# Half-block weight loads behind each early pair, four-tick pairs, ungated loads for the third batch, and two queues for the last stores

## The chip, the cores and the metric

One Trainium2 chip, one of its cores. The metric is the device time of one execution in microseconds (us), as the median of several runs. One execution of the kernel before was also recorded by the hardware profiler; every duration in this document that is not a run's time comes from that record or from the record of an experiment.

The engines are named as the profile names them: PE (TensorE, matmuls), PEld (its weight loads), DVE (VectorE), ACT (ScalarE), POOL (GpSimd) and SP (SyncE, which here only issues transfers).

## The reference, cut to what matters

Two layers are fused. The first is attention over 8 batches with 8 heads, a sequence of 576 and a head width of 64. Heads 0 to 3 use a local mask, heads 4 to 7 a strided one:

```python
rel = pos[:, None] - pos[None, :]
mask_local = (rel >= 0) & (rel < 32)
mask_strided = (rel >= 0) & (pos[None, :] % 32 == pos[:, None] % 32)
attn = softmax(where(mask, q @ k.T / 8, -1e9)); x = attn @ v
```

The heads are laid side by side as x of 576 x 512. The second layer mixes along the sequence with a rank of 32, then along the channels:

```python
u = x + (x.T @ U @ V).T
out = u + relu(u @ w_ch1) @ w_ch2        # 512 -> 2048 -> 512
```

U, V, w_ch1 and w_ch2 arrive as float64 and are turned into float32 on the chip.

## The kernel before, in words

**The main stage.** The output rows are cut into nine pieces of 512: the first 512 rows of each of the eight batches, and a ninth piece made of the 64 last rows of all eight. For each piece the 2048 hidden channels are walked in 16 blocks of 128, so there are 144 steps. A step's first product (`gemm1`, L633) makes one 128 x 512 block of hidden values `ph` from 12 matmuls; ACT and DVE split its relu into a high part `gh` (L637) and a low part `gl` (L638); the second product (`gemm2`, L650) adds 12 matmuls to four accumulators `acc`. The loop runs `gemm1` of the next block before `gemm2` of the last, so each step is 24 matmuls. Work for the next batch is slipped in by `advance`, in half-steps called slots, 32 to a piece.

**The weights.** Block `fc` of both weight matrices is one load of 128 x 1024 float64 words (1 MB, `load_weights`, L155): columns 0 to 511 are what `gemm1` needs, columns 512 to 1023 what `gemm2` needs. `weights` (L171) converts it: `to_f32` scales the high words on ACT (L123) and puts the bits together on DVE (L125, L126, L128), into a buffer `cv`; then ACT writes the high part (L183) and DVE the low part (L184). The first five blocks (`N_FIRST`) are converted during the early attention, in two halves of one load. Each load of blocks 1 to 6 is held back by `load_behind` (L165): a one-word copy on POOL (L159) from a pair's probabilities into the load's buffer makes the load wait for that pair's exponential.

**The early attention.** Batches 0 and 1 (`NSP` is 2) are computed before the main stage by `first_attention` (L549) as eight pairs of heads (pairs 0 to 3 are batch 0, in the order 2, 3, 0, 1 of head pairs). A pair (`early_pair`, L215) loads `qk` and `v`, makes the scores on PE (L323, L329), subtracts the row maximum on DVE (L338, L339), takes the exponential on ACT (L343), transposes it on PE and copies it out on ACT (L350, L353, the tile `PT`), multiplies by v on PE (L363) and normalises on DVE (L372 to L379). For batch 0 it then runs `quarter` (L252): transposes of x, the rank-32 product and its split on PE, ACT and DVE, ending in `uh` and `ul` (L286, L287), the inputs of `gemm1`. The pairs are staggered by ticks, five to a pair of batch 0 and four to a pair of batch 1. All of it shares three banks of PSUM that are handed round. The four `quarter`s of batch 1 run inside the first steps of the main stage.

**The third batch and those after it.** For batches 2 to 7 the local heads run on PE inside the steps (`local_pairs`), and the strided heads on POOL and DVE (`strided_heads`, L404): 27 products on POOL (L422), each reduced on DVE (L424), a softmax, and 27 more products (L450) with their reductions (L452). `S0` names the slot in which a batch's strided heads begin. ACT then copies the result into place (L467, L471), after which SP loads the next batch's `st` into the same buffer (L408). Each instruction queue runs in order, so a `gl` that stands behind a reduction on DVE waits for that reduction's POOL product. For the third batch, `load_qk` and `load_v` hold the loads back by a one-word POOL copy (L201, L208).

**The end.** `finish` (L653) adds the accumulators to u on DVE (L656) and stores the result. For the ninth piece these are eight stores of 64 rows, all issued by SP.

The order on each engine is not written out by hand: a scheduler places the instructions as they are traced, `tc.issue_after` adds an order on one engine (the engine of the named instruction) and nothing between engines.

Of the kernel before, what the change touches and what calls it, by code (L numbers as in the profile page):

```python
# [22 lines left out]
CLA = 5  # L23
N_FIRST = 5
# [4 lines left out]
S0 = {2: 12, **{b: 32 * (b - 1) - 12 for b in range(3, 8)}}  # L29
# [6 lines left out]
def fused_kernel(ctx, tc, pairs, strided, U, V, w_in, masks, eye, out):  # L36
# [126 lines left out]
    gates = {}  # L163

    def load_behind(fc, word):  # L165

# [4 lines left out]
    def weights():  # L171
        for fc in range(NFC):
            load_ahead(fc + 1)
            cv = half_buffer(1024, "cv")
# [4 lines left out]
            fv = cv.rearrange("p (i x) -> p i x", i=2)
            yield  # L180
            parts = w_parts[fc] = const.tile([128, 2, 2, 512], F32R, name=f"w{fc}", tag=f"w{fc}")
            for x in range(2) if fc < N_FIRST else [slice(0, 2)]:
# [1 line left out]
                nc.vector.tensor_tensor(out=parts[:, x, 1], in0=fv[:, x], in1=parts[:, x, 0].bitcast(F32), op=ALU.subtract)  # L184
            yield
# [624 lines left out]
```

## Time and profile before

| What | Value |
|---|---|
| Median of 3 runs (lowest to highest) | 947.96 us (947.95 to 948.24) |
| The profiled execution's own time | 945.37 us |
| Its span, first to last instruction | 943.6 us |
| Mean granted TensorE clock | 0.992 |
| PE busy | 908.2 us, 96% of the span |
| PEld, DVE, ACT, POOL busy | 728.1, 562.0, 244.6, 325.2 us |
| Moved by transfers | 74.24 MB, 79 GB/s over the span |
| First-product matmuls L633 (1152 + 576), mean of one | 393 and 392 ns |
| Second-product matmuls L650 (1152 + 576), mean of one | 392 and 393 ns |

Matmuls overlap, so the mean of one is longer than the distance from one to the next. A row of the timeline gives a start, a duration, engine, line, operation and tiles, and in brackets the idle time before it with what ended it. The stretches view gives, for each window of time, the busy time of each engine, then the granted clock, the share of time that the 16 DMA engines were busy, and GB/s. A row of the chain of waits is a start, a duration and what the end of the program waited for at that moment.

### The profile page before, as it was taken

To read this page: it belongs to the slowest core of one execution; us is meant where nothing else is said; L and a number is where in the kernel's file an instruction comes from. 1 tells how busy PE (TensorE), PEld (TensorE's weight loads), DVE (VectorE), ACT (ScalarE), POOL (GpSimd) and SP (SyncE) were. 2 spreads that over 40 slices of the span, in tenths; PEclk is the share of its full clock that TensorE was granted. 3 is DMA by queue.
4 is the path that set the end of the run, shared out by engine and by line. 5 is a ranking of instruction groups with operands and counts; after the bars stand their busy time and mean duration, and the time that the engine had idled before them with its cause. 6 is when DMAs were issued, how large, how long until landed. Compare 5 with 4: busy or idle time off the path is not lost.

```text
span 943.6 us, 16802 instructions
## 1 busy us (share of the span) xinstructions
PE 908.2 (96%) x7032; PEld 728.1 (77%) x7032; DVE 562.0 (60%) x899; ACT 244.6 (26%) x481; POOL 325.2 (34%) x364
## 2 busy tenths in 40 slices
PE   5878999999989999999999999999999999999996
PEld 3656788777867778777887888778877888888885
DVE  4697997756786678666776677657764341122111
ACT  3454451214122412142114221421242121121110
POOL 0213307333853376346644565447440000000000
PEclk9998999999999999999999999999999999999998
DMA  9978001200240014101420142013300230001001
GB/s 349 382 248 325 1 26 62 96 1 8 74 164 24 12 59 161 49 1 58 139 71 1 51 156 72 1 51 106 112 2 1 56 114 22 0 1 46 1 1 45
DMA packets 35772, 74.24 MB, mean 79 GB/s; under 512 B 5840, under 2 KB 20560, under 8 KB 32880
## 3 DMA queue, kind: packets, MB, share of 16 engines
q1 hardware_dynamic: 25776, 67.13, 20.3%
q10 hardware_dynamic: 8960, 3.68, 1.6%
q0 software_dynamic: 960, 2.36, 0.8%
q8 instruction: 55, 0.90, 0.4%
q14 instruction: 21, 0.17, 0.1%
HBM read 54.14 MB, written 11.67 MB: 70 GB/s over the span
## 4 chain that ended last, share of the span: by engine, by line
PE 88%; DVE 5%; POOL 3%; DMA 1%; ACT 1%; issue 1%; SPq 0%; DVEq 0%; POOLq 0%; ACTq 0%
PE acc L650 40%; PE ph L633 39%; POOL tmp L422 3%; PE px L363 1%; PE px L329 1%; PE px L350 1%; DVE st L452 1%; DMA xg<-in_U_dram 1%; PE px L493 1%; DMA st<-in_strided_dram 1%; PE px L516 1%; PE acc L299 0%; PE px L299 0%; DVE late L339 0%; PE px L265 0%
## 5 line engine op out<-in xcount | busy, mean ns | idle before, releaser
L633 PE MATMUL ph<-uh,w 128*128 128x512 f32 x1152 | 383.3, 393 | 0.0
L650 PE MATMUL acc<-w,gh 128*128 128x512 f32 x1152 | 354.1, 392 | 0.0
L633 PEld LDWEIGHTS ph<-uh,w 128*128 128x128 f32 x1152 | 216.7, 188 | 47.2 <-issue 0.8
L650 PEld LDWEIGHTS acc<-w,gh 128*128 128x128 f32 x1152 | 215.5, 188 | 45.4
L638 DVE SCALAR_TENSOR_TENSOR gl<-ph,gh 128x512 fp32r<-128x512 f32 x144 | 98.7, 687 | 227.4 <-ACT gh L637 226.9
L633 PE MATMUL ph<-ul,w 128*128 128x512 f32 x576 | 225.9, 392 | 0.0
L650 PE MATMUL acc<-w,gl 128*128 128x512 f32 x576 | 219.9, 393 | 2.8 <-DVE gl L638 2.8
L637 ACT ACTIVATE gh<-ph 128x512 fp32r<-128x512 f32 x144 | 85.8, 597 | 469.7 <-PE ph L633 377.8
L450 POOL TENSOR_TENSOR tmp<-st,s_st 128x448 f32<-128x448 f32 (+7 forms) x162 | 136.5, 871 | 185.6 <-DVE st L452 98.6
L422 POOL TENSOR_TENSOR tmp<-st 128x576 f32<-128x576 f32 (+6 forms) x162 | 171.3, 1092 | 79.5 <-DMA st<-in_strided_dram 57.2
L452 DVE TENSOR_REDUCE st<-tmp 128x64 f32<-128x64 f32 (+8 forms) x162 | 137.4, 880 | 15.5 <-POOL tmp L450 14.3
L650 PEld LDWEIGHTS acc<-w,gl 128*128 128x128 f32 x576 | 108.1, 188 | 27.4 <-DVE gl L638 4.0
L633 PEld LDWEIGHTS ph<-ul,w 128*128 128x128 f32 x576 | 108.6, 189 | 22.8
L424 DVE TENSOR_REDUCE s_st<-tmp 128x9 f32<-128x576 f32 (+6 forms) x162 | 87.6, 563 | 24.5 <-POOL tmp L422 23.5
L467 ACT COPY xg<-st 32x256 f32<-32x256 f32 x96 | 38.8, 404 | 7.3 <-DVE st L452 5.8
L504 DVE TENSOR_TENSOR ta<-px,ta 32x256 f32<-32x256 f32 x36 | 15.1, 420 | 35.5 <-ACT ta L502 34.7
L656 DVE TENSOR_TENSOR xg<-acc,xg 128x512 f32<-128x512 f32 x36 | 22.9, 681 | 9.6 <-PE acc L650 9.6
L183 ACT CAST w<-cv 128x1024 fp32r<-128x1024 f32 (+1 forms) x21 | 17.3, 846 | 20.5 <-DVE cv L128 20.4
L625 DVE TENSOR_TENSOR ul<-raw,uh 128x512 fp32r<-128x512 f32 x32 | 20.8, 675 | 2.7 <-ACT uh L624 2.7
L518 DVE TENSOR_TENSOR xg<-px,xg 128x512 f32<-128x512 f32 x24 | 15.4, 685 | 11.6 <-PE px L516 11.6
L126 DVE SCALAR_TENSOR_TENSOR cv<-w,cv 128x1024 int32<-128x1024 int32 (+1 forms) x21 | 21.7, 1042 | 0.2
L184 DVE TENSOR_TENSOR w<-cv,w 128x1024 fp32r<-128x1024 f32 (+1 forms) x21 | 19.8, 962 | 2.6 <-ACT w L183 2.6
(152 smaller groups left out, 488.4 us busy)
## 6 DMA issues: line engine op xcount, KB each, us to landing
w<-in_w_dram SPq DMA_DIRECT2D x16, 1024.0 KB, 10.8
out_dram<-xg SPq DMA_DIRECT2D x32, 256.0 KB, 2.0
v<-in_pairs_dram SPq DMA_DIRECT2D x12, 585.0 KB, 5.0
st<-in_strided_dram SPq DMA_DIRECT2D x6, 1152.0 KB, 5.5
qk<-in_pairs_dram SPq DMA_DIRECT2D x12, 576.0 KB, 5.1
late<-in_pairs_dram SPq DMA_DIRECT2D x8, 585.0 KB, 9.0
late<-in_pairs_dram SPq DMA_DIRECT2D x8, 576.0 KB, 10.6
raw<-bt SPq DMA_DIRECT2D x112, 32.0 KB, 1.9
```

The lines of the kernel that those rows point to most:

```text
L126: nc.vector.scalar_tensor_tensor(out=i, in0=hi_w, scalar=-0x80000000, in1=i, op0=ALU.bitwise_and, op1=ALU.bitwise_or)
L422: nc.gpsimd.tensor_tensor(out=tmp[:, 0:n], in0=sk[:, j0:j0 + n], in1=sq[:, i:i + 1].broadcast_to([128, n, D]), op=ALU.mult)
L424: late.append(lambda tmp=tmp, n=n, i=i, j0=j0: nc.vector.tensor_reduce(out=s_st[:, i, j0:j0 + n], in_=tmp[:, 0:n], axis=AX.X, op=ALU.add))
L450: nc.gpsimd.tensor_tensor(out=tv, in0=sv[:, 0:i + 1, d0:d0 + step], in1=s_st[:, i, 0:i + 1].broadcast_to([128, i + 1, step]), op=ALU.mult)
L452: late.append(lambda tv=tv, i=i, d0=d0, step=step: nc.vector.tensor_reduce(out=o_st[:, i, d0:d0 + step], in_=tv.rearrange("p j d -> p d j" ...
L467: nc.scalar.copy(out=xg[32 * i4:32 * i4 + 32, :, cs], in_=o_st[rows, i4:16:4, :])
L625: nc.vector.tensor_tensor(out=lo, in0=raw[:, :, :, dc, :], in1=hi.bitcast(F32), op=ALU.subtract)
L633: nc.tensor.matmul(ph, w_parts[fc][:, 0, part, 128 * dc:128 * dc + 128], ut[:, dc, :], start=(dc == dcs[0] and i == 0), stop=(dc == dcs[-1 ...
L637: nc.scalar.activation(out=gh, in_=ph, func=AF.Relu)
L638: low = nc.vector.scalar_tensor_tensor(out=gl, in0=ph, scalar=0.0, in1=gh.bitcast(F32), op0=ALU.max, op1=ALU.subtract)
L650: nc.tensor.matmul(accs[n][s // 2][:, s % 2, :], gt[:, cs], w_parts[fc][:, 1, part, :], start=(fc == 0 and i == 0 and n >= NSP), stop=(fc ...
L656: nc.vector.tensor_tensor(out=ot, in0=accs[n][s // 2][:, s % 2, :], in1=ot, op=ALU.add)
```

## The change

It has six parts.

1. **Half-block units.** Blocks 0 to 6 are loaded and converted as two units of 512 columns each, `a` for `gemm1` and `b` for `gemm2`, in the order 0a, 1a, 2a, 3a, 0b, 4a, 1b, 5a, 2b, 6a, 3b, 4b, 5b, 6b; blocks 7 to 15 stay whole. Units 0 and 1 are issued among the first four pairs' loads; behind each pair's exponential from the third pair on, two more units are released by one-word POOL copies. Six units (`N_FIRST`) are converted ahead of the main stage in program order, and in it a block is converted four steps ahead instead of five (`CLA`). Loads of blocks 8 to 15 are now held back too, by a word of a unit converted nine units earlier.
2. **Order on the engines.** The DVE part of a conversion stands behind a pair's subtraction (L339 before) and no longer its ACT part behind a pair's exponential. The conversion of U and V stands behind the first pair's `PT` copy on ACT. A pair's scores stand behind the last product with v on PE.
3. **Four ticks.** The yield between exponential and transposes is gone, so a pair of batch 0 takes four ticks and a pair of batch 1 three.
4. **The third batch's loads** lose their POOL copies. The load of `st` is put inside an `issue_after` on the tenth `gl`, which is a DVE instruction, while the load is issued by SP.
5. **Strided heads of the third batch** begin at slot 20 instead of 12.
6. **The last stores** of 64 rows alternate between SP's queue and ACT's.

```diff
-CLA = 5
-N_FIRST = 5
+CLA = 4
+N_FIRST = 6
+N_LEAD = 4
-S0 = {2: 12, **{b: 32 * (b - 1) - 12 for b in range(3, 8)}}
+S0 = {2: 20, **{b: 32 * (b - 1) - 12 for b in range(3, 8)}}
...
+        with tc.issue_after(marks["PT"][0]):
+            f = to_f32(words_in, early, 128, 10 * R)
...
     def load_weights():
-        for fc in range(NFC):
-            raws[fc] = const.tile([128, 1024], I64, name=f"w{fc}", tag=f"w{fc}")
-            if fc in gates:
-                nc.gpsimd.tensor_copy(out=raws[fc].bitcast(F32)[0:1, 0:1], in_=gates[fc])
-            dma(out=raws[fc], in_=w_in[128 * fc:128 * fc + 128, :])
+        for i, (fc, x) in enumerate(units):
+            n = 1024 if x is None else 512
...
+            if i > N_HALF:
+                gates[i] = word_of[i - N_HALF + BEHIND]
+            if i in gates:
+                nc.gpsimd.tensor_copy(out=raws[i].bitcast(F32)[0:1, 0:1], in_=gates[i])
+            c0 = 512 if x else 0
+            dma(out=raws[i], in_=w_in[128 * fc:128 * fc + 128, c0:c0 + n])
+    lead = [(fc, 0) for fc in range(N_LEAD)]
+    for fc in range(NFC // 2 - 1):
+        lead += [(fc, 1)] + [(fc + N_LEAD, 0)] * (fc + N_LEAD < NFC // 2 - 1)
...
     def load_behind(k, word):
-        if 0 < fc < NFC // 2 - 1:
-            gates[fc] = word
-            load_ahead(fc + 1)
+        if k > 1:
+            for i in (2 * k - 2, 2 * k - 1):
+                gates[i] = word
+                load_ahead(i + 1)
...
+            if i < N_HALF:
+                behind = marks["less"][min(7, i + 2)]
+            else:
+                behind = marks["gl"][fc - BEHIND]
...
     def load_qk(b, pr):
-        if b == NSP:
-            nc.gpsimd.tensor_copy(out=qk[0:1, 0:1], in_=raw[0:1, 0, 0, ORDER1[1], 0:1])
...
-        sp = scores(kT, qT, mask_s if by_class else mask_l)
+        before = marks.get("PV", [])
+        with tc.issue_after(before[-1]) if before else nullcontext():
+            sp = scores(kT, qT, mask_s if by_class else mask_l)
         s_sb = yield from probabilities(sp)
-        load_behind(len(marks["exp"]) - 2, s_sb[0:1, 0, 0, 0:1])
-        yield
+        load_behind(len(marks["exp"]) - 1, s_sb[0:1, 0, 0, 0:1])
...
-        dma(out=st, in_=strided[b - NSP, :, 0:2 * NCH * D])
+        with tc.issue_after(marks["gl"][9]):
+            dma(out=st, in_=strided[b - NSP, :, 0:2 * NCH * D])
...
-                    dma(out=out[2 * s + bb, 512:576, :], in_=ot[64 * bb:64 * bb + 64, :])
+                    (od_dma if bb else dma)(out=out[2 * s + bb, 512:576, :], in_=ot[64 * bb:64 * bb + 64, :])
```

Line numbers move; where the order of the changed program is shown, L346, L367, L380 are the scores, transposes and products with v of a pair (before L329, L350, L363), L652 and L669 the two products (before L633, L650), L657 is `gl` (before L638), L470 the second reductions of the strided heads (before L452).

PE before, around the last two products with v (`w_1044` and `w_1058` are blocks 1 and 2, `w_1072` is block 3; `late` holds the pairs' tiles):

```order
L633 MATMUL ph<-uh,w_1044 128x512 x2
L633 MATMUL ph<-ul,w_1044 128x512
L633 MATMUL ph<-uh,w_1044 128x512
L350 MATMUL px<-ident,late 128x128 x4
L350 MATMUL px<-ident,late 128x64
L363 MATMUL acc<-late 32x65 x80
L633 MATMUL ph<-uh,w_1058 128x512
L633 MATMUL ph<-ul,w_1058 128x512
L633 MATMUL ph<-uh,w_1058 128x512 x2
```

Here 80 matmuls of L363, two pairs' products with v, stand in one row, ahead of the first products of block 2.

PE now, up to the last product with v (`w2a` and `w3a` are the first halves of blocks 2 and 3):

```order
L652 MATMUL ph<-ul,w2a 128x512
L652 MATMUL ph<-uh,w2a 128x512
L652 MATMUL ph<-uh,w3a 128x512
L652 MATMUL ph<-ul,w3a 128x512
L652 MATMUL ph<-uh,w3a 128x512 x2
L652 MATMUL ph<-ul,w3a 128x512
L652 MATMUL ph<-uh,w3a 128x512 x2
L652 MATMUL ph<-ul,w3a 128x512
L652 MATMUL ph<-uh,w3a 128x512 x2
L652 MATMUL ph<-ul,w3a 128x512
L652 MATMUL ph<-uh,w3a 128x512
L380 MATMUL acc<-late 32x65 x40
```

The first products of blocks 2 and 3 stood behind the last two pairs' products with v, which followed each other directly; now the first products of blocks 0 to 3 all stand ahead of the last pair's.

DVE before, at the end of the third batch's strided heads, between the first and the second half of its mixing (`ta`, L504):

```order
L504 TENSOR_TENSOR ta<-px,ta 32x256 x2
L452 TENSOR_REDUCE st<-tmp 128x32
L504 TENSOR_TENSOR ta<-px,ta 32x256
L452 TENSOR_REDUCE st<-tmp 128x32
L508 TENSOR_TENSOR tst<-ta,tst 32x256
L452 TENSOR_REDUCE st<-tmp 128x32 x2
L638 SCALAR_TENSOR_TENSOR gl<-ph,gh 128x512
L452 TENSOR_REDUCE st<-tmp 128x32 x4
L638 SCALAR_TENSOR_TENSOR gl<-ph,gh 128x512
```

All eight second reductions are placed by the second `gl` shown.

DVE now, at the same place (`ta` is L522):

```order
L522 TENSOR_TENSOR ta<-px,ta 32x256 x2
L470 TENSOR_REDUCE st<-tmp 128x32
L522 TENSOR_TENSOR ta<-px,ta 32x256
L470 TENSOR_REDUCE st<-tmp 128x32 x2
L526 TENSOR_TENSOR tst<-ta,tst 32x256
L470 TENSOR_REDUCE st<-tmp 128x32 x2
L657 SCALAR_TENSOR_TENSOR gl<-ph,gh 128x512
L470 TENSOR_REDUCE st<-tmp 128x32 x5
L657 SCALAR_TENSOR_TENSOR gl<-ph,gh 128x512
L470 TENSOR_REDUCE st<-tmp 128x32 x2
L657 SCALAR_TENSOR_TENSOR gl<-ph,gh 128x512
```

Eight reductions followed the first half of the mixing; now twelve do, and one more `gl` stands among them.

More of the change, by code (lines that the diff above doesn't have):

```diff
@@ L137, in small_weights @@
         yield
-        f = to_f32(words_in, early, 128, 10 * R)
+        with tc.issue_after(marks["PT"][0]):
+            f = to_f32(words_in, early, 128, 10 * R)
         nc.scalar.copy(out=U_sb.rearrange("p t r -> p (t r)"), in_=f[:, 0:5 * R])
         nc.scalar.copy(out=U_c.rearrange("p t r -> p (t r)"), in_=f[:, 5 * R:10 * R])
-        f = to_f32(words_in[0:R, 10 * R:10 * R + S], att([128, 640], "cu"), R, S)
+        with tc.issue_after(marks["PT"][0]):
+            f = to_f32(words_in[0:R, 10 * R:10 * R + S], att([128, 640], "cu"), R, S)
         nc.scalar.copy(out=Vst[0:32], in_=f)
@@ new lines, in fused_kernel, with load_behind @@
+    gates, word_of = {}, {}
+    lead = [(fc, 0) for fc in range(N_LEAD)]
+    for fc in range(NFC // 2 - 1):
+        lead += [(fc, 1)] + [(fc + N_LEAD, 0)] * (fc + N_LEAD < NFC // 2 - 1)
+    N_HALF = len(lead)
+    units = lead + [(fc, None) for fc in range(NFC // 2 - 1, NFC)]
+    def load_behind(k, word):
+        if k > 1:
+            for i in (2 * k - 2, 2 * k - 1):
+                gates[i] = word
+                load_ahead(i + 1)
+    def weights():
+        for i, (fc, x) in enumerate(units):
+            load_ahead(i + 1)
+            n = 1024 if x is None else 512
+            cv = half_buffer(n, "cv")
+            if i < N_HALF:
+                behind = marks["less"][min(7, i + 2)]
+            else:
+                behind = marks["gl"][fc - BEHIND]
+            with tc.issue_after(behind):
+                to_f32(raws[i], cv, 128, n)
+            yield
+            tag = f"w{fc}" if x is None else f"w{fc}{'ab'[x]}"
+            parts = const.tile([128, n // 512, 2, 512], F32R, name=tag, tag=tag)
+            for y in range(n // 512):
+                w_parts[fc, y if x is None else x] = parts[:, y]
+            fv = cv.rearrange("p (i x) -> p i x", x=512)
+            nc.scalar.copy(out=parts[:, :, 0], in_=fv)
+            nc.vector.tensor_tensor(out=parts[:, :, 1], in0=fv, in1=parts[:, :, 0].bitcast(F32), op=ALU.subtract)
+            word_of[i] = parts[0:1, 0, 0, 0:1]
@@ L190, in load_ahead @@
     def load_ahead(n):
-        while wl["n"] < min(n, NFC):
+        while wl["n"] < min(n, len(units)):
             next(wl["gen"])
@@ L564, in first_attention @@
                 next(sw)
-        load_ahead(1)
-        for tick in range(len(heads) + 4):
+            if k > 1:
+                load_ahead(k - 1)
+        for tick in range(len(heads) + 3):
             for k in range(len(heads)):
-                if 0 <= tick - k < (4 if k > 3 else 5):
+                if 0 <= tick - k < (3 if k > 3 else 4):
                     next(heads[k], None)
-            for k in (tick, tick - 3):
+            for k in (tick, tick - 2):
                 if 0 <= k < 4:
@@ L575, in first_attention @@
         ring.clear()
-        load_ahead(NFC // 2 - 1)
+        load_ahead(N_HALF + 1)
     def attention(b):
@@ L632, in gemm1 @@
             for i, (part, ut) in enumerate(((0, uh), (0, ul), (1, uh))):
-                nc.tensor.matmul(ph, w_parts[fc][:, 0, part, 128 * dc:128 * dc + 128], ut[:, dc, :],
+                nc.tensor.matmul(ph, w_parts[fc, 0][:, part, 128 * dc:128 * dc + 128], ut[:, dc, :],
                                  start=(dc == dcs[0] and i == 0), stop=(dc == dcs[-1] and i == 2))
@@ L649, in gemm2 @@
             for i, (gt, part) in enumerate(((gh, 0), (gh, 1), (gl, 0))):
-                nc.tensor.matmul(accs[n][s // 2][:, s % 2, :], gt[:, cs], w_parts[fc][:, 1, part, :],
+                nc.tensor.matmul(accs[n][s // 2][:, s % 2, :], gt[:, cs], w_parts[fc, 1][:, part, :],
                                  start=(fc == 0 and i == 0 and n >= NSP), stop=(fc == NFC - 1 and i == 2))
@@ L665, in convert @@
     def convert(n):
-        while counts["conv"] < min(n, 2 * NFC):
+        while counts["conv"] < min(n, 2 * len(units)):
             next(conv)
@@ L671, in fused_kernel @@
     convert(2 * N_FIRST)
+    upto = {fc: max(i for i, u in enumerate(units) if u[0] <= fc) + 1 for fc in range(NFC)}
     banks["prefix"] = False
@@ L724, in fused_kernel @@
         if n == 0:
-            convert(2 * (fc + CLA) + 2)
+            convert(2 * upto[min(NFC - 1, fc + CLA)])
         if len(pend) > 1:
```

18 lines of the change are left out of this document (2 added, 16 removed).

## The prediction

> **What bounds the kernel now.** I read the stretches view first, over the early part of the profiled execution, then the waits and the chain of waits. Columns of the stretches: window, length, busy time of PE, PEld, DVE, ACT and POOL with counts, granted clock, DMA share, GB/s.
>
> ```profile
> core 0: us, PE busy (x) PEld busy (x) DVE busy (x) ACT busy (x) POOL busy (x), PEclk, DMA share, GB/s
> 0.00:20.00 20.00, 9.80 (x312) 6.96 (x312) 8.36 (x14) 7.06 (x11) 0.20 (x4) 1.00 0.92 338
> 20.00:50.00 30.00, 23.54 (x586) 18.05 (x587) 19.07 (x40) 13.37 (x29) 6.73 (x14) 0.94 1.01 378
> 50.00:75.00 25.00, 17.27 (x481) 13.24 (x481) 23.06 (x44) 13.43 (x25) 3.15 (x6) 0.93 0.74 271
> 75.00:94.75 19.75, 19.75 (x87) 15.87 (x88) 13.95 (x25) 8.26 (x12) 8.23 (x13) 0.91 0.84 298
> ```
>
> PE is full from 75 us on. The waits view of the whole span shows, behind that point, one group of PE waits, and it lies between 200 and 300 us:
>
> ```profile
> PE acc L650 <- DVE gl L638: 2.8, 2, 1.8
> ```
>
> So the time is PE's fixed work, plus PE's idle time ahead of 75 us, plus those 2.8 us, plus what follows the last matmul. The change leaves PE's work alone; it can only move idle time. Idle ahead of 75 us: 20 - 9.80 = 10.2, 30 - 23.54 = 6.5 and 25 - 17.27 = 7.7, together 24.4 us. Of the last, 4.3 us are one stop in the middle of the last pair's product with v:
>
> ```profile
> 70.11 4.34 issue
> 74.45 0.45 PE L363 MATMUL acc<-late 64*32 64x65 f32 x10 [4.34 <-issue]
> q8 instruction: 55, 0.90, 0.4%
> ```
>
> PE waited for nothing that the profile shows, with the DMA engines full; since instructions come over those engines too (the third line), I read it as PE waiting for its code. Two stretches also ran at half clock:
>
> ```profile
> 41.00:44.00 3.00, 3.00 (x15) 2.56 (x16) 2.71 (x4) 0.56 (x2) 2.02 (x4) 0.50 0.95 301
> 72.00:78.00 6.00, 3.55 (x18) 2.70 (x18) 6.00 (x13) 2.25 (x3) 1.73 (x4) 0.50 1.01 422
> ```
>
> They cost half of 3.00 and half of 3.55, 3.3 us. As a landmark I take the start of the first product of block 4:
>
> ```profile
> 94.75 0.39 PE L633 MATMUL ph<-uh,w 128*128 128x512 f32 x1
> ```
>
> PE's busy time to there is 9.80 + 23.54 + 17.27 + 19.75 = 70.4, or 67.1 at full clock; 67.1 + 3.3 + 24.4 = 94.8. The same matmuls stand ahead of this landmark after the change, so the early gain is 94.8 less the new sum.
>
> **Part by part: the pairs and the half blocks.** What paced the pairs was DVE together with ACT:
>
> ```profile
> 42.06 0.82 DVE L338 TENSOR_REDUCE mx<-px 128x10 f32<-128x640 f32 x1
> 42.91 0.82 DVE L339 TENSOR_TENSOR late<-px,mx 128x640 f32<-128x640 f32 x1
> 45.12 0.43 DVE L125 TENSOR_SCALAR cv<-cv 128x512 int32<-128x512 int32 x1 [1.38 <-ACT cv L123]
> 45.58 0.69 DVE L126 SCALAR_TENSOR_TENSOR cv<-w,cv 128x512 int32<-128x512 int32 x1
> 46.53 0.69 DVE L128 SCALAR_TENSOR_TENSOR cv<-w,cv 128x512 int32<-128x512 int32 x1
> 47.24 0.28 DVE L274 TENSOR_TENSOR tst<-ph,tst 32x128 fp32r<-32x128 f32 x1
> 48.16 0.16 DVE L372 TENSOR_SCALAR rt<-acc 128x10 f32<-128x10 f32 x1
> 48.89 0.21 DVE L373 RECIPROCAL rt<-rt 128x10 f32<-128x10 f32 x1
> 49.13 0.69 DVE L375 TENSOR_TENSOR xg<-acc,rt 128x512 f32<-128x512 f32 x1
> 49.74 0.27 DVE L379 TENSOR_TENSOR xt<-acc,rt 64x128 f32<-64x128 f32 x1
> 49.94 0.67 DVE L287 TENSOR_TENSOR ul<-acc,uh 128x512 fp32r<-128x512 f32 x1
> 50.54 1.27 DVE L184 TENSOR_TENSOR w<-cv,w 128x512 fp32r<-128x512 f32 x2
> 51.74 0.81 DVE L338 TENSOR_REDUCE mx<-acc 128x10 f32<-128x640 f32 x1
> ```
>
> From one maximum to the next are 9.7 us. A half block costs DVE 0.43 + 0.69 + 0.69 + 0.64 = 2.45, two of them 4.9; the rest is 0.82 + 0.82 + 0.28 + 0.37 + 0.69 + 0.27 + 0.67 = 3.9; and 1.38 is idle, because ACT's part of the conversion stood behind the exponential. With one half per pair and ACT's part free to run early, a tick of DVE is 6.4 and the 1.38 has no cause left.
>
> DVE's own sum from the first normalisation, at 20.3 in the row below, to the last: six pairs' maximum and subtraction, 9.8; eight normalisations of 1.33, 10.6; four quarters of 0.95, 3.8; conversions, eight halves whole and three in part (two lack the last step, one has two steps), 19.6 + 3.6 + 1.1 = 24.3; two `gl` and one tail addition, 2.1. That is 50.6, so 70.9 us without a wait.
>
> ```profile
> 20.32 0.82 DVE L375 TENSOR_TENSOR early<-acc,rt 128x640 f32<-128x640 f32 x1
> ```
>
> DVE will wait: the fourth pair's scores now stand behind the first pair's quarter, and the sixth pair's behind the fourth pair's quarter and three matmuls of block 0. I take 4 us, between none and DVE's old idle time in 20 to 50, 30 - 19.07 = 10.9. The last normalisation is then at 74.9. It frees the second accumulator, behind which 14 second-product matmuls of blocks 0 and 1, a quarter's product and 12 of block 2 stand before the landmark: 26 matmuls at 2.72 / 12 (next row) and 0.5, 6.4 us, so 81.3.
>
> ```profile
> 769.44 2.72 PE ph L633 x12
> ```
>
> The same from PE's side. 0 to 20 us stays, since the same pairs' loads decide it: 10.2. 20 to 50: I take 3 of the old 6.5, between 0 and 6.5. Behind that the first products of blocks 0 to 3, 48 matmuls or 10.9 us, fill PE between the pairs, where 24 did; what is left is PE's wait for the last normalisation, 1.7. Code: with the last two products with v no longer back to back and fewer loads queued then, 2 of the old 4.3 (0 to 4.3). Half clock: 1 of 3.3 (0 to 3.3), since the long stops go. 67.1 + 10.2 + 3 + 1.7 + 2 + 1 = 85.0. DVE's 81.3 with the same 3 is 84.3. I take 85.0: **9.8 us gained**.
>
> What covers the added work: conversions moved into the main stage cost DVE, per whole block, about twice a half, 4.9, and a `gl` of 0.69, 5.6 against PE's 5.44 plus the second batch's quarters, and blocks start several ahead; were that cover gone, each block would cost 0.2. SP's queue passes the wait of a unit's POOL copy with the next unit and pair loads behind it; a pair's v and qk are released earlier than they are used, and the engines move the same bytes as before (338 x 20 + 378 x 30 is 18 MB by 50 us). The copies on POOL (12 and later 8, before 6) sit among transfers it issues and cost 0.2 us each; POOL has 23 of 30 us free. Putting U and V behind the first `PT` moves work of under 1 us on ACT: nothing, within 1 us. Taking the copies off the third batch's loads saves nothing: no PE wait was theirs. The `issue_after` on `st` cannot act, being on another engine's instruction: nothing.
>
> **Part by part: the strided heads of the third batch.** They start eight slots later. This is where the 2.8 us come from; chain of waits and DVE rows:
>
> ```profile
> 228.94 4.40 DVE st L452 x4
> 234.43 5.28 DMA st<-in_strided_dram
> 243.87 23.80 POOL tmp L422 x21
> 209.79 1.89 DVE L452 TENSOR_REDUCE st<-tmp 128x32 f32<-128x416 f32 x2 [1.02 <-POOL tmp L450]
> 213.46 0.96 DVE L452 TENSOR_REDUCE st<-tmp 128x32 f32<-128x448 f32 x1
> ```
>
> The third batch's last reduction frees `st`, the fourth batch's load follows, and then 27 products, all ahead of a `gl`. In the new order four more reductions (two of 416, two of 448) and a `gl` stand behind the first mixing: 1.89 + 2 x 0.96 + 0.69 = 4.5, with the third batch's second mixing two thirds of a step (3.6 us) later on PE. The chain had no slack, so PE's 2.8 grows by this: **4.0 us lost**, bounds 0 (if POOL's 27 products overlap better) and 6.
>
> **Part by part: the last stores.**
>
> ```profile
> 934.49 2.48 DVE L656 TENSOR_TENSOR xg<-acc,xg 128x512 f32<-128x512 f32 x4 [3.21 <-PE acc L650]
> 935.21 5.27 SPq L94 DMA_DIRECT2D out_dram<-xg  x8
> 939.00:940.00 1.00, 0.00 (x0) 0.00 (x0) 0.00 (x0) 0.00 (x0) 0.00 (x0) 0.50 0.85 201
> 279.00:280.00 1.00, 1.00 (x6) 0.84 (x5) 1.00 (x3) 0.00 (x0) 0.30 (x1) 1.00 1.06 412
> ```
>
> SP issues one store per 0.66 us, so the eighth goes at 939.8, while its data is ready at 937.0. With two queues the last goes at about 937.1, 2.7 us earlier. The stores of 64 rows moved 201 GB/s; stores of 128 rows, in the last line, 412. Two halves at once can therefore go at twice the rate: I take **2.4 us gained**, between 0.8 (the engines' free 0.15 of 5.3) and 2.7. [...]
>
> **Sum.** Against the profiled execution, 945.37: -9.8 + 4.0 - 2.4 = -8.2, so 937.2. The median of the runs was 2.6 above it, so 939.8.
>
> **The rivals.**
>
> A, chance 0.18: the last stores share what they have. The DMA share of 0.85 speaks for it, the 412 GB/s against. 947.96 - 9.8 + 4.0 - 0.8 = 941.4. [...]
>
> B, chance 0.06, slower: the third batch's strided chain comes late by all of its eight slots, 8 x 2.72 = 21.8 us, and PE pays at the `gl` behind the fourth batch's products. For it: POOL's 23.80 us without a gap. Against: before, most first products of that batch ran late anyway, and the order moves the end by four reductions. 947.96 - 9.8 + 21.8 - 2.4 = 957.6. It decides the sign from a lateness of 9.8 + 2.4 = 12.2 us.
>
> C, chance 0.14: the early idle time only changes its name. Scores behind quarters keep the 6.5 us in 20 to 50, and the code stop returns whole: 3.5 + 2.3 of the gain go, 4.0 is left. 947.96 - 4.0 + 4.0 - 2.4 = 945.6. For it: the sixth pair's scores stand behind more PE work than before; against: DVE has 2.45 us less per pair.
>
> **How the numbers follow.** The forecast has 0.62 and gives 939.8. The range takes in A and C and the bounds of the early gain: 933 (idle, code and half clock all near their lower bounds) to 946. About 0.2% of this time, 1.9 us, is what a measurement can tell from none. Faster: forecast, A and a little under half of C, 0.86; the same: the rest of C, 0.08; slower: B, 0.06.
>
> **What would show it.** Right: the first product of block 4 starts at 83 to 87; the stop of 4.3 us is gone; the waits view puts 6 to 8 us on PE for `gl` between 200 and 300 us; the last store is issued within 0.5 us of the last addition. Wrong: a landmark past 91 (C), or PE waits of more than 12 us for `gl` (B), or new PE waits for a converted half block in the first ten steps, which I have at nothing; then the time is outside the range.

## The result and the profile after

The changed kernel took 940.89 us (median of 4 runs, 940.06 to 941.39), the kernel before 947.96 (945.64 to 948.24): a ratio of 0.9944, 95% interval 0.9928 to 0.9959. Measured once more beside later experiments it came to 940.65 us and 0.9934 (0.9913 to 0.9954). The forecast was 939.8 us, in a range of 933 to 946, and faster.

The profiled execution took 940.45 us against 945.37, and its span is 938.7 against 943.6, 4.9 us shorter. The prediction's sum for this pair was 8.2. So the time was hit and the gain was not: of the difference to the median, 2.6 us were added in the prediction because the kernel before had run that much above its profiled execution. The changed kernel ran 0.4 above its own. In the 66 runs of the kernel before that stand beside the experiments its median was 947.0 (944.13 to 951.32), so 947.96 was itself a little high; from 947.0 to the 940.7 of all ten runs of the changed kernel are 6.3 us.

Three places split the 4.9. First the early part, in the stretches view of the changed kernel, with the row of the landmark behind it:

```profile
0.00:20.00 20.00, 10.20 (x312) 6.89 (x312) 8.03 (x14) 7.45 (x13) 0.21 (x4) 1.00 0.91 340
20.00:50.00 30.00, 23.81 (x547) 18.24 (x547) 18.50 (x37) 13.58 (x29) 8.12 (x16) 1.00 0.97 341
50.00:75.00 25.00, 23.66 (x549) 17.64 (x550) 21.05 (x40) 11.53 (x19) 7.86 (x18) 0.93 0.53 173
75.00:87.40 12.40, 11.68 (x60) 9.05 (x59) 12.26 (x26) 7.40 (x14) 1.65 (x5) 1.00 0.97 378
87.39 0.39 PE L652 MATMUL ph<-uh,w4a 128*128 128x512 f32 x1
```

The first product of block 4 starts at 87.39 instead of 94.75: 7.4 us gained. PE's idle time went from 10.2, 6.5 and 7.7 to 9.8, 6.2 and 1.3, and 0.7 behind 75 us. What shrank is the last part; the stop of 4.34 us is gone and PE works between the last pairs. The 20 to 50 us stretch kept its idle time.

Second, from the landmark to the last matmul. The first row is the kernel before, the second the changed one, each from its landmark to the last matmul:

```profile
94.75:935.30 840.55, 837.76 (x5568) 673.99 (x5566) 495.86 (x780) 202.46 (x408) 306.93 (x328) 1.00 0.16 50
...
87.40:932.40 845.00, 839.79 (x5568) 675.48 (x5566) 500.13 (x791) 207.25 (x412) 307.87 (x332) 1.00 0.17 56
```

For the same 5568 matmuls it took 4.45 us longer: idle 2.8 became 5.2, and the busy time itself grew by 2.0. The timeline of PE shows where, and the stretch behind it the clock:

```profile
253.12 0.39 PE L543 MATMUL px<-tst,Vst 96*64 96x512 f32 x1
255.93 0.43 PE L340 MATMUL px<-masks_sb 128*128 128x320 bf16 x2 [2.43 <-DVE xt L549]
256.10 1.73 PE L669 MATMUL acc<-w,gh 128*128 128x512 f32 x4
259.81 0.79 PE L669 MATMUL acc<-w,gl 128*128 128x512 f32 x1 [1.98 <-DVE gl L657]
...
256.50:263.40 6.90, 4.92 (x13) 3.33 (x12) 4.19 (x7) 0.60 (x1) 6.90 (x6) 0.51 0.23 57
```

Two stops, 2.43 and 1.98 us, and 6.9 us at half clock with them. The first has a new name: PE waits for `xt`, the addition on DVE that empties the buffer `px`. Its row on DVE, and PE's rows at the same place in the kernel before:

```profile
255.21 0.67 DVE L549 TENSOR_TENSOR xt<-px,xt 64x512 f32<-64x512 f32 x1
...
257.32 0.39 PE L525 MATMUL px<-tst,Vst 96*64 96x512 f32 x1
260.31 0.45 PE L323 MATMUL px<-masks_sb 128*128 128x320 bf16 x2
```

`xt` is no later than it was: it starts 2.1 us behind the product that fills `px` (253.12, L543), and in the kernel before 2.2 us (259.50, behind 257.32). What changed is PE's order. Before, twelve first products stood between the filling of `px` and its next use and covered the wait; now the next use follows at once.

Third, the end. The last matmul, the stores of the two queues, and the stretch in which they move:

```profile
932.06 0.39 PE L669 MATMUL acc<-w,gl 128*128 128x512 f32 x1
932.30 2.48 SPq L95 DMA_DIRECT2D out_dram<-xg  x4
932.31 2.76 ACTq L98 DMA_DIRECT2D out_dram<-xg  x4
934.00:936.00 2.00, 0.00 (x0) 0.00 (x0) 0.07 (x1) 0.00 (x0) 0.00 (x0) 0.95 0.95 317
```

From the start of the last matmul to the end of the span are 6.6 us, before they were 8.6: 2.0 gained. So 7.4 - 4.45 + 2.0 = 4.9.

### The profile page after: what moved, and what is told of

It is laid out like the page before. It is cut to its first block, busy times and chain, and to the rows that moved or that the text cites. A ratio compares the mean times of both kernels' runs of the same rounds, so it can differ in the third digit from the quotient of the medians.

```text
span 938.7 us, 16860 instructions
## 1 busy us (share of the span) xinstructions
PE 909.2 (97%) x7032; PEld 727.3 (77%) x7032; DVE 561.6 (60%) x907; ACT 247.2 (26%) x485; POOL 325.7 (35%) x374
## 4 chain that ended last, share of the span: by engine, by line
PE 83%; DVE 6%; POOL 5%; DMA 3%; issue 2%; ACT 1%; SPq 0%; DVEq 0%; POOLq 0%
PE acc L669 38%; PE ph L652 37%; POOL tmp L440 5%; DVE st L470 1%; PE px L380 1%; DMA w1a<-in_w_dram 1%; PE px L346 1%; PE px L367 1%; DMA w2a<-in_w_dram 1%; DMA late<-in_pairs_dram 1%; PE px L511 1%; DMA st<-in_strided_dram 1%; DVE gl L657 1%; PE px L534 1%; DVE s_st L442 0%
## 5 line engine op out<-in xcount | busy, mean ns | idle before, releaser
L657 DVE SCALAR_TENSOR_TENSOR gl<-ph,gh 128x512 fp32r<-128x512 f32 x144 | 98.8, 688 | 224.2 <-ACT gh L656 223.6
L652 PE MATMUL ph<-uh,w 128*128 128x512 f32 x648 | 215.0, 392 | 0.0
L669 PE MATMUL acc<-w,gh 128*128 128x512 f32 x648 | 197.6, 393 | 0.0
L470 DVE TENSOR_REDUCE st<-tmp 128x64 f32<-128x64 f32 (+8 forms) x162 | 137.6, 882 | 15.4 <-POOL tmp L468 14.3
L669 PEld LDWEIGHTS acc<-w,gh 128*128 128x128 f32 x648 | 122.2, 189 | 25.6
L652 PEld LDWEIGHTS ph<-uh,w 128*128 128x128 f32 x648 | 121.3, 188 | 26.4 <-issue 0.4
L652 PE MATMUL ph<-ul,w 128*128 128x512 f32 x324 | 126.8, 391 | 0.0
L669 PE MATMUL acc<-w,gl 128*128 128x512 f32 x324 | 122.2, 393 | 2.1 <-DVE gl L657 2.0
L669 PEld LDWEIGHTS acc<-w,gl 128*128 128x128 f32 x324 | 61.4, 189 | 16.7 <-DVE gl L657 3.2
L652 PEld LDWEIGHTS ph<-ul,w 128*128 128x128 f32 x324 | 60.8, 188 | 12.9
L522 DVE TENSOR_TENSOR ta<-px,ta 32x256 f32<-32x256 f32 x36 | 15.1, 420 | 33.1 <-ACT ta L520 32.3
L652 PE MATMUL ph<-uh,w6a 128*128 128x512 f32 x72 | 25.1, 398 | 0.0
L652 PE MATMUL ph<-uh,w0a 128*128 128x512 f32 x72 | 24.8, 403 | 0.0
L652 PE MATMUL ph<-uh,w1a 128*128 128x512 f32 x72 | 24.1, 391 | 0.0
L652 PE MATMUL ph<-uh,w5a 128*128 128x512 f32 x72 | 23.8, 391 | 0.0
```

Of the source, the lines that this page charges most:

```text
L470: late.append(lambda tv=tv, i=i, d0=d0, step=step: nc.vector.tensor_reduce(out=o_st[:, i, d0:d0 + step], in_=tv.rearrange("p j d -> p d j" ...
L522: nc.vector.tensor_tensor(out=ta, in0=ps_a[32 * j:32 * j + 32, :], in1=ta, op=ALU.add)
L652: nc.tensor.matmul(ph, w_parts[fc, 0][:, part, 128 * dc:128 * dc + 128], ut[:, dc, :], start=(dc == dcs[0] and i == 0), stop=(dc == dcs[-1 ...
L657: low = nc.vector.scalar_tensor_tensor(out=gl, in0=ph, scalar=0.0, in1=gh.bitcast(F32), op0=ALU.max, op1=ALU.subtract)
L669: nc.tensor.matmul(accs[n][s // 2][:, s % 2, :], gt[:, cs], w_parts[fc, 1][:, part, :], start=(fc == 0 and i == 0 and n >= NSP), stop=(fc ...
```

## Experiments

My theory of the 4.45 us was the later start of the third batch's strided heads, the rival the shorter early part. My theory of the early gain was the half blocks on DVE, the rival the ticks. The versions with slot 8, 12 or 16 also leave out the order on `st`, which changes no instruction on any engine. Medians and ratios to the kernel before:

| Kernel | us (runs) | ratio, interval |
|---|---|---|
| changed, slot 12 | 938.14 (6) | 0.9915, 0.9898 to 0.9932 |
| changed, slot 16 | 940.11 (6) | 0.9936, 0.9922 to 0.9951 |
| changed, last stores on SP | 941.99 (6) | 0.9952, 0.9937 to 0.9968 |
| changed, five ticks | 944.47 (12) | 0.9977, 0.9962 to 0.9991 |
| before, slot 20 | 949.36 (12) | 1.0024, 1.0007 to 1.0040 |
| before, four ticks | 948.77 (12) | 1.0019, 1.0003 to 1.0035 |
| changed, slot 8 | 942.00 (10) | 0.9949, 0.9929 to 0.9969 |
| changed, longer waits for gl | 945.05 (1) | none |
| changed, again | 940.65 (6) | 0.9934, 0.9913 to 0.9954 |
| changed, slot 12, end at 16 | 933.87 (4) | 0.9855, 0.9839 to 0.9871 |
| changed, slot 12, one unit | 943.72 (11) | 0.9963, 0.9947 to 0.9979 |
| changed, slot 12, behind exp | 948.61 (12) | 1.0013, 1.0000 to 1.0025 |

**The later start.** Slot 12 in the changed kernel:

```diff
-S0 = {2: 20, **{b: 32 * (b - 1) - 12 for b in range(3, 8)}}
+S0 = {2: 12, **{b: 32 * (b - 1) - 12 for b in range(3, 8)}}
```

> The changed kernel with the third batch's strided heads begun at slot 12 again (the order on st, which acts on nothing, is left out). Behind the first product of block 4 the changed kernel spends 845.0 us where the one before spent 840.55: PE idle 5.2 instead of 2.8, and 2.0 more of busy time, most of it at half clock between 256.5 and 263.4. Theory: all of this comes from the later start. Then the idle goes back to about 2.8, no stretch at half clock is left behind 100 us, and the time is 940.9 - 4.4 = 936.5. Rival: the later start was not the cause but the shorter early part, which leaves the chain of POOL products fewer us before the place where PE needs it; then slot 12 gains less than 1 us, 940 to 941, or new gl waits come in the steps where quarters and conversions share DVE, 941 to 943.

Its PE timeline at the same place, and the stretch behind the second wait:

```profile
257.56 0.50 PE L669 MATMUL acc<-w,gl 128*128 128x512 f32 x1 [0.91 <-DVE gl L657]
265.13 0.50 PE L669 MATMUL acc<-w,gl 128*128 128x512 f32 x1 [1.81 <-DVE gl L657]
...
265.20:272.20 7.00, 7.00 (x31) 5.81 (x32) 6.23 (x15) 1.91 (x4) 3.00 (x6) 1.00 0.70 283
```

These are the waits of before, 0.93 and 1.82, and the clock stays at 1.00; the wait for `xt` is gone, since PE's order has the first products behind the filling of `px` again (252.31 to 255.29). 2.75 us were gained of the 4.4 expected. The theory holds; the early part, whose stops differ from execution to execution, blurs the size.

> The same with slot 16, half way. Theory of lateness slot by slot: the loss is smaller by about half, or all of it is gone if PE's two waits stay too short to bring the half clock: 936.5 to 939. Rival (shorter early part): 940 to 941.

The same edit with 16. PE's timeline at that place, and the clock behind it:

```profile
256.60 0.43 PE L340 MATMUL px<-masks_sb 128*128 128x320 bf16 x2 [2.28 <-DVE xt L549]
266.52 0.80 PE L669 MATMUL acc<-w,gl 128*128 128x512 f32 x1 [3.09 <-DVE gl L657]
...
265.90:272.70 6.80, 6.18 (x15) 4.88 (x16) 5.82 (x14) 2.54 (x5) 2.10 (x5) 0.50 0.80 325
```

Both waits and the half clock are there, so nothing of the loss is saved; the median of 940.11 lies within the scatter of the changed kernel. The loss isn't linear in the slots: it comes with the wait for `xt`. Here seven of the twelve first products still stand between the filling of `px` (252.54) and its next use, but `xt` starts 3.3 us behind the filling instead of 2.2, after a reduction that waited 0.81 us for POOL. The other side, slot 20 in the kernel before:

```diff
-S0 = {2: 12, **{b: 32 * (b - 1) - 12 for b in range(3, 8)}}
+S0 = {2: 20, **{b: 32 * (b - 1) - 12 for b in range(3, 8)}}
```

> The kernel before with nothing but the third batch's strided heads begun at slot 20 instead of 12. Theory: the later start by itself brings the wait of PE for the copy of xt behind the fourth batch's reductions, the longer wait for gl and the stretch at half clock that follows them, which cost 2.8 us in the changed kernel against its version with slot 12: 2 to 4.5 us over the kernel before, a ratio of 1.002 to 1.005, with a stretch at half clock between 250 and 275 us. Rival: it takes the shorter early part as well; then within 0.1% of the kernel before and no such stretch.

```profile
262.80 0.69 PE L323 MATMUL px<-masks_sb 128*128 128x320 bf16 x2 [2.88 <-DVE xt L531]
266.66 0.79 PE L650 MATMUL acc<-w,gl 128*128 128x512 f32 x1 [1.46 <-DVE gl L638]
...
261.80:272.00 10.20, 7.74 (x19) 5.55 (x19) 6.64 (x11) 0.60 (x1) 9.85 (x8) 0.50 0.24 52
```

The same two waits and 10.2 us at half clock, with the old early part; here too the next use of `px` follows its filling (259.53) at once. The rival falls: the later start alone costs 2.3 us here (0.7 to 3.8).

> The changed kernel with slot 8 (the order on st left out). With slot 12 two waits of PE for gl are left, 0.91 and 1.81 us at 257 and 265. Theory of lateness: the chain comes four slots earlier and they go: 2 to 3 us under slot 12, 935.5 to 936.5. Rival: POOL's first products collide with its transfers for batch 1, or DVE's reductions with the conversions of the first ten steps, so that nothing is gained or new waits come: 938 to 941.

Slot 8 (the same edit in the changed kernel) lost 3.9 us against slot 12. Its trace has waits that slot 12 lacks or has shorter, in the first steps and at the end of the chain:

```profile
104.38 0.50 PE L669 MATMUL acc<-w4b,gl 128*128 128x512 f32 x1 [1.86 <-DVE gl L657]
...
270.26 0.50 PE L669 MATMUL acc<-w,gl 128*128 128x512 f32 x1 [2.76 <-DVE gl L657]
...
270.80:274.20 3.40, 3.40 (x9) 2.63 (x8) 3.40 (x9) 1.44 (x3) 0.00 (x0) 0.50 1.03 424
```

The rival is right: the start isn't what sets the end of the chain. The end itself does. `S1` names the slot by which a batch's strided heads are to end; its first number is for the third batch alone:

```diff
-S0 = {2: 20, **{b: 32 * (b - 1) - 12 for b in range(3, 8)}}
+S0 = {2: 12, **{b: 32 * (b - 1) - 12 for b in range(3, 8)}}
-S1 = (20, 14)
+S1 = (16, 14)
```

> The changed kernel with slot 12 (the order on st left out), and the third batch's strided heads to end four slots earlier as well (S1 16 instead of 20). Left with slot 12 were two waits of PE for gl, 0.91 and 1.81 us at 257 and 265 us, ahead of which stand the third batch's last reductions, the load of st and 27 products of POOL without a gap. Theory: that end sets them, four slots are 11 us, and both go: 2.7 us less than with slot 12, about 935.4. Rival: DVE and POOL can't be denser there (POOL waits up to 10.8 us for DVE in that stretch), the end moves little, and new waits for gl come before 230 us: 937 to 940.

```profile
229.69 27.77 POOL L440 TENSOR_TENSOR tmp<-st 128x64 f32<-128x64 f32 x27 [7.98 <-DMA st<-in_strided_dram]
...
200.00:300.00 100.00, 100.00 (x753) 79.95 (x752) 68.99 (x115) 25.81 (x56) 50.78 (x55) 1.00 0.20 64
...
25.40:925.00 899.60, 890.25 (x6699) 714.43 (x6699) 548.36 (x884) 236.71 (x467) 325.92 (x366) 1.00 0.21 71
```

POOL's 27 products start at 229.69, in the version with slot 12 they start at 234.81. PE has no idle time left between 200 and 300 us, and the clock reads 1.00 from 25.4 to 925 us. 933.87 us beats both kernels. It is 4.3 us under slot 12, more than the 2.7 of waits; its profiled execution also had no half clock in the early part.

**The last stores.**

```diff
-                    (od_dma if bb else dma)(out=out[2 * s + bb, 512:576, :], in_=ot[64 * bb:64 * bb + 64, :])
+                    dma(out=out[2 * s + bb, 512:576, :], in_=ot[64 * bb:64 * bb + 64, :])
```

> The changed kernel with the eight last stores all issued by SP again. From the start of PE's last matmul to the end of the span were 8.6 us before and 6.6 in the changed kernel. Theory: issue by one queue set the end, so the time is 2.0 longer, 942.9. Rival: the engines moved the stores no faster from two queues, and the 2.0 come from elsewhere: at most 0.8 longer, 941.7 or less.

```profile
931.83 0.39 PE L669 MATMUL acc<-w,gl 128*128 128x512 f32 x1
932.07 5.03 SPq L95 DMA_DIRECT2D out_dram<-xg  x8
934.00:936.00 2.00, 0.00 (x0) 0.00 (x0) 0.00 (x0) 0.00 (x0) 0.00 (x0) 1.00 0.88 205
```

The median is 1.1 above the changed kernel's. From the last matmul's start to the end of the span (939.8) are 7.9 us. In all traces here two queues took 6.4 to 6.6 (ten traces), and one queue 8.6 three times and 7.9 here. So the second queue is worth 1.3 to 2.2 us; the rate was 317 GB/s instead of 205. The 205 is the rate of issue: eight stores of 128 KB in 5.03 us are 208 GB/s.

**The ticks.** Five ticks in the changed kernel:

```diff
         load_behind(len(marks["exp"]) - 1, s_sb[0:1, 0, 0, 0:1])
+        yield
...
-        for tick in range(len(heads) + 3):
+        for tick in range(len(heads) + 4):
...
-                if 0 <= tick - k < (3 if k > 3 else 4):
+                if 0 <= tick - k < (4 if k > 3 else 5):
...
-            for k in (tick, tick - 2):
+            for k in (tick, tick - 3):
...
-            if tick in (1, 2):
+            if tick in (2, 3):
```

> The changed kernel with the yield between exponential and transposes put back, five ticks for a pair of batch 0 and four for batch 1, the loads of the pairs three ticks ahead as before, and U and V one tick later. The early gain is 7.3 us at the first product of block 4 (94.75 to 87.4). Theory: half blocks on DVE carry it, and the ticks only move PE's work between pairs: 940 to 943, landmark within 2 us of 87.4. Rival: the ticks carry it, since they put a pair's transposes and products ahead of the next pair's scores: 946 to 948, landmark at 92 to 95.

```profile
51.50:61.70 10.20, 8.95 (x53) 6.63 (x54) 2.38 (x6) 2.45 (x5) 1.34 (x2) 0.50 0.52 170
```

3.6 to 3.8 us lost, between the two; half of the early gain. Much of it can be the half clock: 8.95 us of PE's work ran in these 10.2 us, where the changed kernel has one stretch of 3.4. The runs bear it out: the median of their granted clocks is 0.987, the changed kernel's 0.993, and the one of the twelve at 0.993 took 940.49 us. Four ticks alone, in the kernel before (the first four edits turned round):

> The kernel before with nothing but four ticks for a pair of batch 0 and three for batch 1. Putting five ticks back into the changed kernel cost it 3.6 us. Theory: ticks and half blocks add up, so the ticks alone give 2 to 4 us: a ratio of 0.996 to 0.998. Rival: with whole blocks to convert behind a pair (DVE 4.9 us, ACT behind the exponential) DVE still paces the pairs and the ticks alone give under 1 us, or lose, a ratio of 0.999 or more.

```profile
52.78 0.79 PE L275 MATMUL acc<-Vst,tst 96*128 96x512 f32 x1 [4.06 <-DVE tst L273]
...
69.79 0.50 PE L632 MATMUL ph<-uh,w 128*128 128x512 f32 x1 [1.99 <-ACT w L183]
...
76.83 1.42 PE L362 MATMUL acc<-late 64*32 64x65 f32 x80 [3.12 <-ACT late L352]
```

They lose 1.7 us: with whole blocks, DVE and ACT are late for everything that PE now reaches sooner. Ticks and half blocks don't add up: alone the ticks lose.

**ACT's part of the conversion.** In the changed kernel with slot 12:

```diff
-                behind = marks["less"][min(7, i + 2)]
+                behind = marks["exp"][min(7, i + 2)]
```

> The changed kernel with slot 12, and the conversion's part on ACT again behind the exponential of a pair, DVE's part free. Theory of the prediction: DVE then waits for ACT in the middle of the pairs, 1.38 us a pair as before the change, four to six pairs, and part of it reaches PE: 1 to 3 us over slot 12, 939 to 941. Rival: DVE was idle for 11.5 us of 20 to 50 anyway and the pairs are paced through PE's code stops and the hand-over of banks, so nothing changes: 937.5 to 938.7.

```profile
22.49 0.43 DVE L126 TENSOR_SCALAR cv<-cv 128x512 int32<-128x512 int32 x1 [1.36 <-ACT cv L124]
...
53.51 0.43 DVE L126 TENSOR_SCALAR cv<-cv 128x512 int32<-128x512 int32 x1 [1.35 <-ACT cv L124]
...
55.90 0.28 DVE L291 TENSOR_TENSOR tst<-ph,tst 32x128 fp32r<-32x128 f32 x1
...
56.23 0.73 PE L293 MATMUL acc<-Vst,tst 96*128 96x512 f32 x1 [4.93 <-DVE tst L291]
```

10.5 us over slot 12, the largest single cost found, far more than either side expected, and more than the whole early gain. DVE's 1.36 us waits are back; behind them stands `tst`, for which PE waits 4.93 us. The edit also delays later steps: PE is idle 5.75 us between 100 and 300 us, where slot 12 has 3.5.

Idle time is the smaller part of the loss, though. From start to end PE is idle 4.4 us longer than with slot 12, and the two spans differ by 10.8. Most of the rest goes with the half clock: ahead of PE's last matmul this trace holds 20.5 us of it in three stretches, slot 12's 3.4 in one; the second of the three follows the stop of 4.93:

```profile
56.30:63.20 6.90, 6.90 (x19) 4.88 (x20) 2.50 (x5) 1.50 (x3) 1.34 (x2) 0.51 0.34 113
```

No run has whole blocks with ACT's part free, so what the half blocks bring apart from it is not shown.

**PE's stops without a name.** Counted over PE's matmuls, its weight loads and its sequencer's own instructions, the stops of its matmuls called "issue" stand behind the 449th, 705th, 1985th and 2753rd in the kernel before (0.61, 1.13, 0.94 and 4.34 us) and behind the 449th, 1473rd and 1729th in the changed kernel (2.04, 1.84 and 2.30 us): 449 plus multiples of 256 each time. Neither trace has another of over 0.25 us; with slot 12 there is one more, of 1.26 us at 61.57, behind the 2241st. The instruction queue moved 55 transfers and 0.90 MB in the kernel before, 16 KB each, and the record holds 14133 instructions of PE, 257 to a transfer by estimate. From these numbers I read the stops as reads of code, which the prediction had taken from one stop; no run shows it directly. Behind 88 us each of the two traces passes 44 more such places without a stop of over 0.1 us; ahead of 75 us, among the loads, the stops were of up to 4.34. I tried to shorten them by queueing less:

```diff
-            for i in (2 * k - 2, 2 * k - 1):
+            for i in (k,):
```

> The changed kernel with slot 12, and one half unit released behind a pair's exponential instead of two. Theory: PE's stops without a named cause come 256 PE instructions apart (the 449th, 1473rd, 1729th, 2241st), so they are reads of its code, and their length comes from the transfers queued then; with less queued the DMA share of 20 to 50 us falls from 0.94 to 0.8 or less and the stops behind 20 us shrink from 4.25 us to under 2.5: 936 to 937, unless the later halves make PE wait for converted weights. Rival: a read of code takes that long by itself, the stops stay at about 4, and the later loads cost: 939 to 944.

This didn't do what it should. Units that were no longer released by a pair were held back by nothing, and a block of 1152 KB of `st` went out among the pairs' loads; the transfers of 20 to 50 us with one unit, then those with two:

```profile
DMA packets 2986, 11.66 MB, mean 389 GB/s; under 512 B 423, under 2 KB 423, under 8 KB 2853
...
DMA packets 2623, 10.08 MB, mean 336 GB/s; under 512 B 402, under 2 KB 402, under 8 KB 2520
```

More moved, not less, and 5.6 us were lost. What sets the length of a code stop stays open: the one behind the 1473rd instruction took 1.13 us (last stores on SP) to 2.33 (slot 8) in kernels whose order on PE is the same up to it.

**Waits for the clock.** `gl` was written several times in seven steps of the last two pieces:

```diff
+    REPS = {112: 5, 116: 6, 120: 7, 124: 8, 129: 9, 134: 10, 139: 12}
...
+        for _ in range(REPS.get(step, 0)):
+            nc.vector.scalar_tensor_tensor(out=gl, in0=ph, scalar=0.0, in1=gh.bitcast(F32), op0=ALU.max, op1=ALU.subtract)
```

> The changed kernel with gl written several times over, the same values, in seven steps of the last two pieces, where DVE is idle 4.75 us of 5.44: 5, 6, 7 and 8 extra times in steps 112, 116, 120, 124 and 9, 10 and 12 in steps 129, 134, 139. At 0.60 us each and with about 2.2 us of slack PE should stop for 0.8, 1.4, 2.0, 2.6, 3.2, 3.8 and 5.0 us. Theory: a stop of PE by its length alone brings the half clock, from somewhere between 2.04 (a stop at 15.7 us that brought none) and 2.3 us on: stretches of 3.4 or 6.8 us at half clock behind the last four stops and none behind the first three. Rival: the half clock comes from what was around the stops (transfers at full rate, short 64-row matmuls, two stops within 4 us) and these stops, alone among full matmuls, bring none.

```profile
762.86 0.50 PE L654 MATMUL ph<-uh,w2a 128*128 128x512 f32 x1 [1.40 <-DVE gl L661]
```

This was the longest stop of PE in these steps, shorter than I had reckoned, and the clock stayed at 1.00 from 740 to 930 us. So the stops of up to 1.40 us among full matmuls brought no half clock here; on longer ones this tells nothing. This experiment was badly sized; the stops that other traces happened to hold say more (last section).

**The changed kernel again** (no edit).

> The changed kernel itself, beside the next three. The version with slot 12 came to a ratio of 0.9915 to the kernel before, the changed kernel to 0.9944, on different runs. Theory: the difference is real, so this gives 940 to 941.5 and a ratio of 0.993 to 0.996, and its trace again holds the stretch at half clock near 256 us behind the waits for xt and gl. Rival: the two differ by the runs only; then a ratio of 0.992 or less.

The median and the waits repeat. Its profiled execution was the slowest of the six, 945.10 us, and has the same order with another early part:

```profile
92.05 0.39 PE L652 MATMUL ph<-uh,w4a 128*128 128x512 f32 x1
...
45.70:52.50 6.80, 6.79 (x25) 4.73 (x24) 2.35 (x6) 1.79 (x3) 0.00 (x0) 0.50 0.77 246
66.20:69.60 3.40, 3.40 (x73) 2.58 (x62) 1.98 (x5) 1.17 (x3) 1.33 (x2) 0.50 0.81 273
```

The landmark is 4.7 us later than in the first trace, with 10.2 us at half clock instead of 3.4. Two experiments whose edits lie behind the landmark, and whose order ahead of it is the same, have it at 87.10 (last stores on SP) and 83.95 (longer waits for `gl`). So one profiled execution fixes the early part of this kernel only to some microseconds.

## Why the prediction was right, and which of its steps were wrong

- **Early gain, forecast 9.8, measured 7.4.** By the four landmarks of the changed kernel, 83.95 to 92.05, it lies between 2.7 and 10.8, so the forecast is within the scatter. Term by term, the 85.0 of the prediction became 87.4 in this trace. The term that was mis-sized is "Code ... 2 of the old 4.3": 1.84 + 2.30 = 4.1 came. Most of the 6.2 us that PE was idle in 20 to 50, where the prediction took 3, is the same thing: without these stops it is 3.3. The half clock took 1.7 instead of 1, the first 20 us 9.8 instead of 10.2.
- **DVE's wait, forecast 4.** This step failed too. From the first normalisation at 19.39 to the last at 80.24, DVE's rows add up to 49.9 us, close to the 50.6 of the prediction. But rows overlap, as the stretches view shows; DVE was busy for 45.35 us and idle for 15.5. Part of that stands behind the code stops, in pairs of rows of the changed kernel, PE's stop and DVE's idle time behind it:

```profile
19.39:80.24 60.85, 52.45 (x1127) 39.70 (x1125) 45.35 (x88) 28.22 (x53) 17.19 (x36) 0.97 0.78 271
...
41.98 0.66 PE L380 MATMUL acc<-late 64*32 64x65 f32 x40 [1.84 <-issue]
51.21 0.41 PE L346 MATMUL px<-late 64*32 64x64 f32 x18 [2.30 <-issue]
...
42.68 0.17 DVE L389 TENSOR_SCALAR rt<-acc 128x10 f32<-128x10 f32 x1 [1.42 <-PE acc L380]
51.68 0.82 DVE L355 TENSOR_REDUCE mx<-px 128x10 f32<-128x640 f32 x1 [3.07 <-PE px L346]
```

- **Code.** The stop behind the 2753rd instruction went, and two others came inside the pairs, where DVE waits for PE. Rival C had this right, that the code returns whole; the rest of the idle time in 20 to 50 did shrink, from 5.3 to 3.3. In these traces the stops stand multiples of 256 instructions apart; what sets their lengths, 0.61 to 4.34 us in the two kernels, was not shown.
- **The last normalisation, 1.7, and the end of the pairs.** PE's idle time behind 50 us was 1.3 + 0.7 = 2.1, of which 1.2 belong to the second code stop; the first products of blocks 0 to 3 do fill it. This step was right, and it is where most of the gain is.
- **DVE's tick, from 9.7 to 6.4, with ACT's part set free.** Right in its direction, and worth more than said: putting ACT's part back costs 10.5 us, the larger part of it with the half clock, of which that trace holds 20.5 us against 3.4 with slot 12. With ACT's part put back the kernel is no faster than the one before (a ratio of 1.0000 to 1.0025), so the rest of the early gain needs it free.
- **The third batch, forecast -4.0, measured -4.45.** The number was hit, the mechanism was not, so this is luck. The lateness came as forecast, 4.4 us for the 4.5: POOL's products for the fourth batch start 149.5 us behind the landmark instead of 145.1. But the sign that I named did not come: PE's waits for `gl` between 200 and 300 us were 2.0, not 6 to 8, less than the 2.8 of before. What came instead is the wait of 2.43 for `xt`, by a change of PE's order there that I hadn't looked at, and about 2 us for half clock, which I had counted in the early part only. By their runs the two experiments put the later start at 2.3 and 2.75 us. Rival B's 21.8 didn't come; lateness isn't handed on slot by slot.
- **The last stores, forecast -2.4, measured -2.0** (1.3 to 2.2 by all traces). Right; the eighth issue starts at 934.51, 0.45 us behind the end of the last addition. Rival A's 0.8 is too little. The 205 GB/s of one queue were its rate of issue, so the 317 of two show only that the engines had room left. With two queues a store took 2.7 and 3.2 us (the medians of the queues) from issue to landing, with one 2.3.
- **Edits at nothing.** PE has 0.6 us of waits between 87 and 250 us, so conversions in the first steps cost next to nothing. Two edits are no edits: with and without the order on `st`, and with and without the scores put behind the last product with v, the order on every engine is the same.
- **The median.** The 2.6 us between profile and median were scatter, not a constant to be added: of the 66 runs, the five at the profile's granted clock, 0.992, took 944.7 to 945.3 us, as the profiled execution did, and the median of all was at 0.988. They made up for most of a gain that was 3.3 too large on the profiled pair. The range held because it was built from the bounds; the point is luck to that extent.

## What to carry to other kernels

When a step is moved, compare the order on every engine around it, and not only on the one whose wait the profile already names; here PE's order closed up, and laid bare a wait that other work had covered. The end of a chain, moved four slots earlier, was worth more than all that was tried with its start. Parts of a change that pace the same engines don't add up: shorter ticks lost time alone and gained with half blocks. And take a difference of a few us in a part that waits for transfers from several executions, not from one.

## What the runs showed of the hardware

In these traces the half clock follows a pattern that I had not expected to find. In the kernel before, the clock is at half from 41.00 to 44.41 us, from 71.72 to 78.55 and again from 938.70, behind the last matmul; in the changed kernel from 51.73 to 55.15, from 256.53 to 263.36 and again from 935.79. From one change to the next are 1, 8, 2 and 252 times 3.41 us in the first trace, 1, 59, 2 and 197 times in the second. I divided the two records along this grid and added up PE's idle time in each piece of 3.41 us that ran at full clock, between 30 and 925 us. Four pieces were followed by half clock; they held 1.55 us (37.58) and 2.08 (68.30) in the kernel before, 2.30 (48.32) and 2.43 (253.12) in the changed one. The most that any other piece held was 1.69 (64.89 in the kernel before), then 1.35. So the pieces ahead of half clock are among those with the most idle time, but one at 1.55 was followed by it and one at 1.69 was not. How long the half clock then lasts, one piece or two, this doesn't tell.

Nor did the length of one stop decide it in these traces. The kernel before and the kernel before with four ticks have nearly the same stop, 1.82 and 1.83 us; behind the first the clock stays at 1.00, the second is followed by half clock:

```profile
270.16 0.50 PE L650 MATMUL acc<-w,gl 128*128 128x512 f32 x1 [1.82 <-DVE gl L638]
...
270.20:277.20 7.00, 7.00 (x31) 5.76 (x32) 5.96 (x14) 1.95 (x4) 2.96 (x6) 1.00 0.71 294
...
272.47 0.50 PE L649 MATMUL acc<-w,gl 128*128 128x512 f32 x1 [1.83 <-DVE gl L637]
...
273.50:276.90 3.40, 3.40 (x10) 2.62 (x9) 2.94 (x8) 0.95 (x2) 0.36 (x2) 0.51 1.02 420
```

The grid of the first trace has an edge at 269.69, which cuts the stop: 1.35 us of it lie ahead of the edge and 0.47 behind. All of the second stop lies in the 3.41 us ahead of 273.50. So nearly the same stop brought no half clock in one trace and, by estimate, cost half of 3.40 us more, 1.7, in the other; where a stop falls may thus be part of the scatter between executions.
